# One core, attention and two expert layers: the attention stage's DMA issues put in another order

## The chip, the core and the metric

The kernel runs on one core of a Trainium2 chip, in one launch. The core has five engines, each with an instruction stream of its own that it works off strictly in order: TensorE (PE, matmuls; its weight loads are listed as PEld), VectorE (DVE), ScalarE (ACT), GpSimd (POOL) and SyncE (SP), which here does nothing but issue DMAs. They wait for one another and for DMAs at semaphores. A DMA is issued by SP and then moved by 16 DMA engines on their own; while SP waits for what one DMA needs, all DMAs behind it in its stream wait too. The metric is the device time of one execution in microseconds. Three runs of the kernel before took 801.37, 802.45 and 802.65 us; the median is 802.45.

## The reference

Attention over clusters, then two expert layers on its output, all in float32. Sizes: batch 2, 8 heads, 768 positions, head dimension 64, 16 centroids per head.

```python
q_assign = argmax(q_n @ c_n^T)        # cluster of each query, by normalised vectors
k_assign = argmax(k_n @ c_n^T)        # cluster of each key
scores = where(q_assign == k_assign, q @ k^T / sqrt(64), -1e9)
attn = exp(scores - max(scores)); attn /= sum(attn) + 1e-9
x = attn @ v                          # heads side by side: 1536 tokens x 512
h = x @ w_in                          # 512 -> 2048
x = ((a0 + a1 h + a2 h^2 + a3 h^3) / (1 + |b0||h| + |b1| h^2 + 1e-6)) @ w_out
x = (silu(x @ w_gate) * (x @ w_val)) @ w_o2       # 512 -> 1536 -> 512
```

## The kernel before, in words

Three stages follow one another: attention (the first 255 us of the profiled span), the first expert layer, the second expert layer. The change lies in attention alone.

Attention works on pairs of heads, 8 of them (`pairs`). A pair has 12 steps: 2 halves of the queries, 3 blocks of 128 queries in each, 2 heads. The main loop (line 617) runs over all 96 steps n; below, s = n mod 12 is the step within a pair and k = n // 12 the pair. All instructions go out in the order in which the loop writes them; the schedule is by hand and nothing reorders it. In each step:

- `scores` (369): four matmuls give 128 x 768 scores. q and k are split into a rounded part and a remainder, and stand in two tiles each: q1 and k1 hold 128 rows, q2 and k2 hold 64 rows of q or k and behind them 16 mask rows, a one-hot of the cluster times a large number, so that the mask comes out of the same matmuls.
- `maximum` (385, DVE) and `exponentials` (392, ACT) read the scores; the sum over each row falls out of the exponential. Two score tiles exist (`ps_s`).
- `transposes` (424, PE) turn the exponentials of earlier steps; ACT and DVE copy them to `pt`.

At steps 2 and 8 a *run* of 24 matmuls (`weighted`, 435) multiplies a finished half with v. It accumulates in `o_ps`, of which there is one only: the next run can't start before `normalised` (445, DVE) has read the last one. `normalised` gives x = o_ps * rb, and stands at step 0 and step 6 (in the first pair one step later). rb holds the reciprocals of the row sums, spread over the partitions. They come by a long way: `reciprocals` (401, DVE) and a transpose to `rs` at steps 2 and 8 (`spread`, 408, PE and ACT), a DMA from rs to a DRAM tile rd (line 415, also steps 2 and 8), and at steps 4 and 10 two DMAs from rd to rb with a broadcast (`bring_back`, 418). The half whose run stands at step 2 gets its reciprocals at step 2, rb at step 4, x at step 6, and the run at step 8 waits for that x.

During a pair the next one is made ready: its queries and keys are rounded and split on POOL (`halves_of`, 584: head one at steps 0 to 3, head two at 4 to 7), its clusters are found on DVE (`chain_of`, 559: steps 8 and 2), and the mask rows t3 are transposed on DVE at step 2 (`to_rows`, 357). Weight blocks for the later stages are loaded and prepared in some steps (`early`, 530).

The order of SP's stream is therefore the order in which these functions are called. Per pair, from the second on:

| step | SP's issues in the kernel before |
|---|---|
| 0 | sq and sk of the pair after next (`load_pair`, 187); q2 <- q1 of head one (273) |
| 2 | eight mask rows t3 -> q2 and k2 (365); rd <- rs (415) |
| 4 | rb <- rd, two (422); in most pairs a weight block (78); q2 <- q1 of head two (273) |
| 8 | rd <- rs |
| 10 | rb <- rd, two; v of both heads (192); q and k of both heads of the pair after next, four (181) |

In the first pair the mask rows go out at step 8 instead of 2, ahead of rd, and `load_pair` at step 4. The last pair has no pair to make ready, and so no mask rows, no rounded queries and no loads of q, k and v.

Of the kernel before, what the change touches and what calls it, by code (L numbers as in the profile page):

```python
# [20 lines left out]
def tile_kernel(ctx, tc, q_t, k_t, q_s, k_s, v_l, cent, w_in, w_out, a_co, b_co, w_gate, w_val, w_o2, out):  # L21
# [17 lines left out]
    def r32(ap):  # L39
        return ap.bitcast(F32)  # L40
# [76 lines left out]
    def block_start():  # L117
        n = len(started)
        if n < len(loads):
            key, f, src = loads[n]  # L120
            started.append(block_load(src[f]))
# [40 lines left out]
    heads = {}  # L162
    live = {}
    pairs = [(b, hp) for b in range(B) for hp in range(H // 2)]
    order = [(b, hp, half, i, e) for b, hp in pairs for half in range(2) for i in range(HB) for e in range(2)]
    PER = 2 * HB
# [5 lines left out]
    def x_tile(key):  # L172
        at = S * (n_x[0] % 6)
        n_x[0] += 1
        return xa[:, at:at + S]

    def load_qk(b, h):
        t = heads.setdefault((b, h), {})
        for key, src in (("xq", q_t), ("xk", k_t)):
            t[key] = x_tile(key)  # L180
            nc.sync.dma_start(out=t[key], in_=src[b, h])


    def load_pair(b, hp, keys=("sq", "sk")):
        for key in keys:
            live[key] = xs_p.tile([P, S], F32, tag=key, name=key)
            nc.sync.dma_start(out=live[key], in_=(q_s if key == "sq" else k_s)[b, hp])

    def load_v(b, h):
        t = heads[b, h]  # L190
        t["v"] = v_p.tile([P, NB, D], F32, tag="v", name="v")
        nc.sync.dma_start(out=t["v"], in_=v_l[b, h])
# [19 lines left out]
    def keep_warm(n, to, x=None):  # L212
        for _ in range(n):
            for j in range(HB):
                nc.tensor.transpose(to[:, j, :], ident if x is None else x[:, 0:P], ident)
# [47 lines left out]
    def tiles_qk(b, h):  # L263
        t = heads[b, h]
        for key in ("q1", "q2", "k1", "k2"):
            t[key] = qk_p.tile([P, S], F32R, tag=key, name=key)

    def q_hi(b, h):
        t = heads[b, h]
        if "q1" not in t:  # L270
            tiles_qk(b, h)
        nc.gpsimd.tensor_scalar(out=t["q1"], in0=t["xq"], scalar1=scale, scalar2=0.0, op0=ALU.mult, op1=ALU.add)
        nc.sync.dma_start(out=r32(t["q2"])[0:D, :], in_=r32(t["q1"])[0:D, :])

    def q_scale(b, h):
# [78 lines left out]
        sm = live["sm"]  # L354
        nc.scalar.activation(out=sm, in_=sm, func=AF.Identity, scale=msk[:, 0:1], bias=msk[:, 1:2])

    def to_rows(b, hp):
        del live["t1"], live["mx"]
        t3 = rb_p.tile([P, HALF], F32, tag="rb", name="t3")
        nc.vector.transpose(out=t3, in_=live.pop("sm").rearrange("p j c -> p (j c)"))  # L360
        for e in range(2):
            for m, key in enumerate(("q2", "k2")):
                for half in range(2):
                    g = 64 * m + 32 * half + NC * e
                    nc.sync.dma_start(  # L365
                        out=r32(heads[b, 2 * hp + e][key])[D:KM, half * HALF:(half + 1) * HALF], in_=t3[g:g + NC, :]
                    )

    def scores(b, hp, half, i, e):
        t = heads[b, 2 * hp + e]  # L370
        s_ps = ps_s.tile([P, S], F32, tag="s", name="s_ps")
        q0 = half * HALF + i * P
        qs = slice(q0, q0 + P)
        for lo, hi in CUT:
            nc.tensor.matmul(s_ps[:, lo:hi], t["q1"][:, qs], t["k1"][:, lo:hi], start=True, stop=False)  # L375
        if (b, hp, half, i, e) == order[0]:
            keep_warm(6, fill, oh[0])
        for lo, hi in CUT:
            nc.tensor.matmul(s_ps[:, lo:hi], t["q2"][0:KM, qs], t["k2"][0:KM, lo:hi], start=False, stop=True)  # L379
        if (i, e) == (0, 0):  # L380
            st = live["st", b, hp, half] = st_p.tile([P, 3, PER], F32, tag="st", name="st")
            nc.vector.memset(st[:, 2, :], 1e-9)
        live["s", b, hp, half, i, e] = s_ps

    def maximum(b, hp, half, i, e):
        st = live["st", b, hp, half]
        k = e * HB + i
        nc.vector.tensor_reduce(  # L388
            out=st[:, 0, k:k + 1], in_=live["s", b, hp, half, i, e], axis=AX.X, op=ALU.max, negate=True
        )  # L390
# [27 lines left out]
    def bring_back(b, hp, half):  # L418
        rd = live.pop(("rd", b, hp, half))
        rb = live["rb", b, hp, half] = rb_p.tile([P, HALF], F32, tag="rb", name="rb")  # L420
        for e in range(2):
            nc.sync.dma_start(out=rb[e * D:(e + 1) * D, :], in_=rd[e:e + 1, :].to_broadcast([D, HALF]))

    def transposes(b, hp, half, i, e, g, copy):
        p = live["p", b, hp, half, i, e] if g == 0 else live.pop(("p", b, hp, half, i, e))
        if (i, g) == (0, 0):
            live["pt", b, hp, half, e] = pt_p.tile([P, NB, HALF], F32, tag="pt", name="pt")
        pt = live["pt", b, hp, half, e]
        t_ps = t_tile("t_ps")
        for j in range(HB):  # L430
            kb = g * HB + j
            nc.tensor.transpose(t_ps[:, j, :], p[:, kb * P:(kb + 1) * P], ident)  # L432
        copy(out=pt[:, g * HB:(g + 1) * HB, i * P:(i + 1) * P], in_=t_ps)  # L433
# [82 lines left out]
    def q_rows(t, half):  # L516
        nc.scalar.activation(
            out=t["q2"][D:D + 32, cols[half]], in_=t["t3"][32 * half:32 * half + 32, :],
            func=AF.Identity, scale=MASKED, bias=msk[32 * half:32 * half + 32, 1:2],
        )  # L520
# [12 lines left out]
    def pair_of(k):  # L533
        b, hp = pairs[k + 1]
        return b, hp, (b, 2 * hp), (b, 2 * hp + 1)

    def loads_of(n):
        k, s = divmod(n, 2 * PER)
        if n == early[0] - 7 or n - 2 in early[:-1]:
            block_start()  # L540
        if s == (0 if k else 4) and k + 2 < len(pairs):
            load_pair(*pairs[k + 2])
        elif s == 10 and k + 1 < len(pairs):
            b, hp, a, c = pair_of(k)
            load_v(*a)
            load_v(*c)
            if k + 2 < len(pairs):
                b, hp = pairs[k + 2]
                load_qk(b, 2 * hp)
                load_qk(b, 2 * hp + 1)  # L550

    def sims_of(n):
        k, s = divmod(n, 2 * PER)
# [25 lines left out]
    def rows_of(n):  # L579
        k, s = divmod(n, 2 * PER)  # L580
        if k + 1 < len(pairs) and (n == 8 or n > 8 and s == 2):
            to_rows(*pairs[k + 1])

    def halves_of(n):
        k, s = divmod(n, 2 * PER)
# [22 lines left out]
    def run_of(m):  # L608
        for _ in range(m):
            if pv:  # L610
                step = pv.pop(0)
                weighted(*step)
                if step[3] == NB - 1:
                    return step[:3]

    finished = done = None
    for n in range(len(order) + 2):
        c = n % PER
        if n < len(order):
            scores(*order[n])  # L620
            maximum(*order[n])
        if n == 1:
            keep_warm(3, fill)
        for j, (lag, g, copy) in enumerate(TURNS[c]):
            if (n, j) == (len(order), 1):
                finished = run_of(NB)
            if n >= lag:
                transposes(*order[n - lag], g, copy)
                if g == 1 and (n - lag) % PER == PER - 1:
                    pv.extend([order[n - lag][:3] + (kb,) for kb in range(NB)])  # L630
        if n < len(order):
            exponentials(*order[n])
        if n == 1:
            q_rows(h1, 1)
            for t in (h0, h1):
                del t["t3"]
        if finished and (n == len(order) + 1 or c == (1 if n < 3 * PER else 0) and n < len(order)):
            normalised(*finished)
            finished, done = None, finished
        if c == RUN and n > PER:  # L640
            reciprocals(*order[n - 3][:3])
        elif n == len(order):
            reciprocals(*order[-1][:3])
        if c == 4 and n > PER:
            bring_back(*order[n - 5][:3])
        loads_of(n)
        sims_of(n)
        if c == RUN:
            finished = run_of(NB if n < LATE else NB // 2)
        if n == 8:  # L650
            rows_of(n)
        if n in early:
            block_shift(started[early.index(n)])
        chain_of(n)
        halves_of(n)
        if done and c == RUN:
            split_x(*done)
            done = None
        block_of(n)
        if n > 8:  # L660
            rows_of(n)
        if c == RUN and n > PER:
            spread(*order[n - 3][:3])
        elif n == len(order) + 1:
            spread(*order[-1][:3])
# [11 lines left out]
    with ExitStack() as mctx:  # L677
# [292 lines left out]
        for n in range(NS):  # L970
            t, f = seq[n][:2]
# [422 lines left out]
        j, c = 2 * u, 2  # L1394
# [61 lines left out]
```

## Time and profile before

| | |
|---|---|
| median of 3 runs | 802.45 us (801.37 to 802.65) |
| the profiled execution | 805.28 us |
| its span, first to last instruction | 803.5 us |
| PE busy | 776.2 us, 97% of the span |
| DVE, ACT, POOL busy | 603.9, 505.5, 455.3 us (75%, 63%, 57%) |
| mean granted TensorE clock | 0.984 of 2.4 GHz |
| mean DMA rate | 85 GB/s |

The profiled execution is one, and its own time is what its span is held against; the timed runs are others. An engine's share over the whole span is a mean over three stages with different limits, so the attention stage is read by itself. A busy PE is one whose matmuls overlap without a gap; it says nothing about the clock, which has a column of its own in the windows. Idle time in front of an instruction is put down to what came last before it started.

### The profile page before, as it was taken

Reading aid. Unit: us, or ns where it says so; the run is one execution under the profiler, and the core shown is the slowest. Engines: PE = TensorE matmul, PEld = TensorE weight load, DVE = VectorE, ACT = ScalarE, POOL = GpSimd, SP = SyncE. Lnnn points to the kernel's source line nnn. Section 1 sums busy time; section 2 is a strip of 40 time slices with the busy share of each in tenths; the row PEclk is TensorE's granted clock in tenths of the full one; section 3 lists DMA queues with packets and bytes.
Section 4 is the critical chain, followed back from the end, with each engine's and each line's share of the span. In section 5 each row is a group of like instructions: output and inputs, shape, how many; then the busy total and the mean of one; then the engine's idle time right before and its main releaser. Section 6 shows DMA issues by size and latency. Waiting matters only on the chain.

```text
span 803.5 us, 11575 instructions
## 1 busy us (share of the span) xinstructions
PE 776.2 (97%) x4119; PEld 646.9 (81%) x4119; DVE 603.9 (75%) x919; ACT 505.5 (63%) x959; POOL 455.3 (57%) x429
## 2 busy tenths in 40 slices
PE   8979889898899999999999999999999999999998
PEld 6756766576676888888888888899999999999997
DVE  6857778587576999988999999998576566656444
ACT  7756666485586778868777777666554544444331
POOL 6473874764922477666777777947344445434310
PEclk9998999899999999999999999999999999999999
DMA  7265354254122212112112111012221213120003
GB/s 218 72 201 180 90 181 162 55 173 160 56 93 73 68 65 78 56 50 79 53 53 78 53 54 52 28 52 80 80 78 56 76 53 106 53 79 27 1 36 122
DMA packets 27209, 67.94 MB, mean 85 GB/s; under 512 B 4464, under 2 KB 10832, under 8 KB 27152
## 3 DMA queue, kind: packets, MB, share of 16 engines
q1 hardware_dynamic: 27152, 67.21, 25.8%
q8 instruction: 32, 0.52, 0.3%
q14 instruction: 25, 0.20, 0.1%
HBM read 59.48 MB, written 3.19 MB: 78 GB/s over the span
## 4 chain that ended last, share of the span: by engine, by line
PE 84%; DVE 5%; ACT 4%; DMA 3%; POOL 2%; issue 1%; SPq 1%; DVEq 0%; POOLq 0%; ACTq 0%
PE c_ps L1046 23%; PE acc L782 14%; PE h_ps L726 14%; PE acc L1103 12%; PE o_ps L439 9%; PE t_ps L432 5%; PE s_ps L375 3%; PE s_ps L379 3%; DMA rb<-rd 2%; DVE st L388 2%; DMA rd<-rs 1%; ACT p L396 1%; POOL tmp L743 1%; DVE x L447 1%; SPq L365 1%
## 5 line engine op out<-in xcount | busy, mean ns | idle before, releaser
L1046 PE MATMUL c_ps<-r,wb 128*128 128x384 f32 x648 | 125.3, 336 | 0.0
L1046 PEld LDWEIGHTS c_ps<-r,wb 128*128 128x128 f32 x648 | 115.4, 188 | 6.0
L388 DVE TENSOR_REDUCE st<-s_ps 128x1 f32<-128x768 f32 x96 | 90.7, 953 | 28.5 <-PE s_ps L379 28.3
L396 ACT ACTIVATE p<-s_ps,st 128x768 f32<-128x768 f32 x96 | 86.9, 906 | 36.5 <-DVE st L388 35.7
L439 PE MATMUL o_ps<-pt,v 128*64 128x384 f32 x384 | 76.6, 552 | 20.0 <-DVE x L447 20.0
L743 POOL TENSOR_TENSOR tmp<-tmp 128x512 f32<-128x512 f32 x46 | 68.1, 1480 | 47.5 <-ACT tmp L742 47.1
L1054 ACT COPY tmp<-c_ps 128x384 f32<-128x384 f32 x60 | 28.9, 481 | 86.9 <-PE c_ps L1046 86.9
L439 PEld LDWEIGHTS o_ps<-pt,v 128*64 128x64 f32 x384 | 34.3, 154 | 58.0 <-issue 30.9
L1125 POOL TENSOR_TENSOR part<-tmp,part 128x512 f32<-128x512 f32 x18 | 23.4, 1298 | 101.2 <-ACT tmp L1124 101.2
L432 PE MATMUL t_ps<-ident,p 128*128 128x128 f32 x576 | 76.3, 272 | 0.5 <-DVE pt L433 0.5
L432 PEld LDWEIGHTS t_ps<-ident,p 128*128 128x128 f32 x576 | 66.0, 140 | 4.8 <-DVE pt L433 0.7
L782 PE MATMUL acc<-g,r 128*128 128x512 f32 x288 | 69.1, 389 | 0.2 <-ACT part L789 0.2
L766 POOL TENSOR_TENSOR g<-td,tmp 128x512 fp32r<-128x512 f32 x45 | 58.6, 1301 | 18.0 <-DVE td L761 18.0
L433 ACT COPY pt<-t_ps 128x384 f32<-128x384 f32 x128 | 56.7, 481 | 16.0 <-PE t_ps L432 13.7
L1057 DVE TENSOR_TENSOR tmp<-tmp,c_ps 128x384 f32<-128x384 f32 x40 | 22.2, 554 | 58.9 <-ACT tmp L1054 45.1
L1046 PE MATMUL c_ps<-r,xw 128*128 128x384 f32 x336 | 65.4, 337 | 0.0
L782 PEld LDWEIGHTS acc<-g,r 128*128 128x128 f32 x288 | 54.0, 188 | 11.8 <-ACT part L789 0.6
L1046 PEld LDWEIGHTS c_ps<-r,xw 128*128 128x128 f32 x336 | 60.0, 188 | 3.7
L726 PE MATMUL h_ps<-r 128*128 128x512 f32 x252 | 60.5, 390 | 0.0
L1103 PE MATMUL acc<-wb,g 128*128 128x512 f32 x216 | 59.4, 394 | 0.0
L375 PE MATMUL s_ps<-k,q 128*128 128x512 f32 x192 | 57.6, 381 | 1.3 <-ACT p L396 1.1
L726 PEld LDWEIGHTS h_ps<-r 128*128 128x128 f32 x252 | 47.1, 188 | 10.3 <-issue 0.6
(169 smaller groups left out, 1793.9 us busy)
## 6 DMA issues: line engine op xcount, KB each, us to landing
raw<-w_in_dram SPq DMA_DIRECT2D x16, 512.0 KB
raw<-w_out_dram SPq DMA_DIRECT2D x16, 512.0 KB
raw<-w_val_dram SPq DMA_DIRECT2D x12, 512.0 KB
raw<-w_gate_dram SPq DMA_DIRECT2D x12, 512.0 KB
raw<-w_o_dram SPq DMA_DIRECT2D x12, 512.0 KB
xa<-q_t_dram SPq DMA_DIRECT2D x14, 384.0 KB
xa<-k_t_dram SPq DMA_DIRECT2D x14, 384.0 KB
sq<-q_s_dram SPq DMA_DIRECT2D x8, 384.0 KB
```

The source lines that it names most:

```text
L375: nc.tensor.matmul(s_ps[:, lo:hi], t["q1"][:, qs], t["k1"][:, lo:hi], start=True, stop=False)
L388: nc.vector.tensor_reduce(out=st[:, 0, k:k + 1], in_=live["s", b, hp, half, i, e], axis=AX.X, op=ALU.max, negate=True)
L396: nc.scalar.activation(out=p, in_=live.pop(("s", b, hp, half, i, e)), func=AF.Exp, bias=st[:, 0, k:k + 1], accum_out=st[:, 1, k:k + 1],)
L432: nc.tensor.transpose(t_ps[:, j, :], p[:, kb * P:(kb + 1) * P], ident)
L433: copy(out=pt[:, g * HB:(g + 1) * HB, i * P:(i + 1) * P], in_=t_ps)
L439: nc.tensor.matmul(live["o", b, hp, half][e * D:(e + 1) * D, :], heads[b, 2 * hp + e]["v"][:, kb, :], live["pt", b, hp, half, e][:, kb, :] ...
L726: nc.tensor.matmul(h_ps, w[:, wi, cs], x[:, xi, cc, :], start=(n == 0), stop=(n == 3 * NCC - 1))
L743: spread.tensor_tensor(out=tq, in0=tq, in1=tr, op=ALU.add)
L766: eng.tensor_tensor(out=g[:, 1, :], in0=td, in1=tr, op=ALU.mult)
L782: nc.tensor.matmul(acc[c], w[:, wi, cs], g[:, gi, :], start=(first and m == 0), stop=(last and m == 2))
L1046: nc.tensor.matmul(live2[key], set_of[f][:, wi, a, cs], x[xi][:, kc, :], start=(first and n == 0), stop=(n == last), skip_group_check=True,)
L1103: nc.tensor.matmul(acc2[j, c], g[:, gi, c * P:(c + 1) * P], w[:, wi, :], start=(f % 2 == 0 and m == 0), stop=(f % 2 == 1 and m == 2),)
```

## The change

`to_rows` is cut in two: the transpose on DVE stays at step 2, and the eight DMAs become `send_rows`, at step 4 behind `bring_back` (in the first pair at step 8 as before). The DMA q2 <- q1 is taken out of `q_hi` and becomes `q_send`, at steps 5 and 9. The loads of q and k of the pair after next are spread: head one at step 5, head two at step 10. A new function `sends_of` is called in each step after `bring_back` and before `loads_of`. No other instruction is touched.

| step | SP's issues in the changed kernel, from the second pair on |
|---|---|
| 0 | sq and sk of the pair after next |
| 2 | rd <- rs |
| 4 | rb <- rd, two; eight mask rows; in most pairs a weight block |
| 5 | q2 <- q1 of head one; q and k of head one of the pair after next |
| 8 | rd <- rs |
| 9 | q2 <- q1 of head two |
| 10 | rb <- rd, two; v of both heads; q and k of head two of the pair after next |

```diff
--- before.py
+++ after.py
@@ -270,6 +270,9 @@
         if "q1" not in t:
             tiles_qk(b, h)
         nc.gpsimd.tensor_scalar(out=t["q1"], in0=t["xq"], scalar1=scale, scalar2=0.0, op0=ALU.mult, op1=ALU.add)
+
+    def q_send(b, h):
+        t = heads[b, h]
         nc.sync.dma_start(out=r32(t["q2"])[0:D, :], in_=r32(t["q1"])[0:D, :])
 
     def q_scale(b, h):
@@ -354,10 +357,14 @@
         sm = live["sm"]
         nc.scalar.activation(out=sm, in_=sm, func=AF.Identity, scale=msk[:, 0:1], bias=msk[:, 1:2])
 
-    def to_rows(b, hp):
+    def to_rows():
         del live["t1"], live["mx"]
         t3 = rb_p.tile([P, HALF], F32, tag="rb", name="t3")
         nc.vector.transpose(out=t3, in_=live.pop("sm").rearrange("p j c -> p (j c)"))
+        live["t3"] = t3
+
+    def send_rows(b, hp):
+        t3 = live.pop("t3")
         for e in range(2):
             for m, key in enumerate(("q2", "k2")):
                 for half in range(2):
@@ -544,10 +551,9 @@
             b, hp, a, c = pair_of(k)
             load_v(*a)
             load_v(*c)
-            if k + 2 < len(pairs):
-                b, hp = pairs[k + 2]
-                load_qk(b, 2 * hp)
-                load_qk(b, 2 * hp + 1)
+        if s in (5, 10) and k + 2 < len(pairs):
+            b, hp = pairs[k + 2]
+            load_qk(b, 2 * hp + (s == 10))
 
     def sims_of(n):
         k, s = divmod(n, 2 * PER)
@@ -579,7 +585,20 @@
     def rows_of(n):
         k, s = divmod(n, 2 * PER)
         if k + 1 < len(pairs) and (n == 8 or n > 8 and s == 2):
-            to_rows(*pairs[k + 1])
+            to_rows()
+        if n == 8:
+            send_rows(*pairs[1])
+
+    def sends_of(n):
+        k, s = divmod(n, 2 * PER)
+        if k + 1 < len(pairs):
+            b, hp, a, c = pair_of(k)
+            if s == 4 and k:
+                send_rows(b, hp)
+            elif s == 5:
+                q_send(*a)
+            elif s == 9:
+                q_send(*c)
 
     def halves_of(n):
         k, s = divmod(n, 2 * PER)
@@ -643,6 +662,7 @@
             reciprocals(*order[-1][:3])
         if c == 4 and n > PER:
             bring_back(*order[n - 5][:3])
+        sends_of(n)
         loads_of(n)
         sims_of(n)
         if c == RUN:
```

## Rows read from the trace of the kernel before

**Rows 1.** The page, costliest groups: busy us, mean ns, idle before, what ended it.

```profile
L439 PE MATMUL o_ps<-pt,v 128*64 128x384 f32 x384 | 76.6, 552 | 20.0 <-DVE x L447 20.0
```

**Rows 2.** Waits over the whole span: us in total, times, longest us.

```profile
POOL q L272 <- DMA xa<-q_t_dram: 58.7, 5, 16.0
...
DVE x L447 <- DMA rb<-rd: 27.3, 6, 5.7
```

**Rows 3.** Timeline of PE: the runs of line 439.

```profile
59.58 6.82 PE L439 MATMUL o_ps<-pt,v 128*64 128x384 f32 x24 [4.31 <-DVE x L447]
...
74.95 4.09 PE L439 MATMUL o_ps<-pt,v 128*64 128x384 f32 x24
...
90.63 4.16 PE L439 MATMUL o_ps<-pt,v 128*64 128x384 f32 x24 [2.25 <-DVE x L447]
...
119.85 5.71 PE L439 MATMUL o_ps<-pt,v 128*64 128x384 f32 x24 [3.08 <-DVE x L447]
...
151.17 7.10 PE L439 MATMUL o_ps<-pt,v 128*64 128x384 f32 x24 [3.63 <-DVE x L447]
...
183.25 5.85 PE L439 MATMUL o_ps<-pt,v 128*64 128x384 f32 x24 [2.95 <-DVE x L447]
...
214.10 5.86 PE L439 MATMUL o_ps<-pt,v 128*64 128x384 f32 x24 [3.56 <-DVE x L447]
...
241.07 2.16 PE L439 MATMUL o_ps<-pt,v 128*64 128x384 f32 x12
```

**Rows 4.** Windows: stretch, length, busy us (count) by engine, PEclk, DMA share, GB/s.

```profile
59.50:66.40 6.90, 6.82 (x26) 3.24 (x26) 5.18 (x11) 2.44 (x5) 3.89 (x7) 0.60 0.01 2
93.00:116.80 23.80, 23.77 (x166) 18.02 (x162) 19.81 (x32) 18.08 (x42) 17.01 (x22) 1.00 0.43 144
38.50:48.00 9.50, 9.29 (x63) 6.26 (x62) 6.87 (x12) 6.52 (x16) 3.15 (x5) 1.00 0.88 311
48.50:51.00 2.50, 2.50 (x20) 2.30 (x19) 2.50 (x5) 2.43 (x7) 2.33 (x4) 1.00 0.99 224
```

**Rows 5.** Timeline of all engines in the third pair, steps 2 to 8.

```profile
79.28 0.26 ACT L413 COPY rs<-r_ps 6x128 f32<-6x128 f32 x1 [0.96 <-PE r_ps L411]
...
87.89 0.49 PE L306 MATMUL sim<-sk,ct 128*32 128x384 f32 x2
...
88.02 0.84 POOL L272 TENSOR_SCALAR q<-xa 128x768 fp32r<-128x768 f32 x1
...
90.02 0.56 DVE L447 TENSOR_TENSOR x<-o_ps,rb 128x384 f32<-128x384 f32 x1 [3.64 <-DMA rb<-rd]
```

**Rows 6.** Timeline of SP in the same stretch.

```profile
80.06 1.19 SPq L365 DMA_DIRECT2D q<-t  x2
...
85.14 0.42 SPq L415 DMA_DIRECT2D rd<-rs  x1
...
86.52 1.12 SPq L422 DMA_DIRECT2D rb<-rd  x2
...
87.69 0.58 SPq L78 DMA_DIRECT2D raw<-w_in_dram  x1
```

**Rows 7.** Timeline of SP: rd at step 8 there, and in the last pair.

```profile
95.32 0.29 SPq L415 DMA_DIRECT2D rd<-rs  x1
...
233.11 0.28 SPq L415 DMA_DIRECT2D rd<-rs  x1
```

**Rows 8.** Timeline of DVE: x of the half with run at step 8.

```profile
102.06 0.55 DVE L447 TENSOR_TENSOR x<-o_ps,rb 128x384 f32<-128x384 f32 x1
```

**Rows 9.** Timeline of DVE: lines 349 and 95 in two places each.

```profile
28.05 1.07 DVE L349 TENSOR_TENSOR sm<-wt,mx 128x384 f32<-128x384 f32 x1
...
43.42 0.56 DVE L349 TENSOR_TENSOR sm<-wt,mx 128x384 f32<-128x384 f32 x1
...
78.34 1.20 DVE L95 SCALAR_TENSOR_TENSOR c<-raw,c 128x512 uint32<-128x512 uint32 x1
...
231.77 0.69 DVE L95 SCALAR_TENSOR_TENSOR c<-raw,c 128x512 uint32<-128x512 uint32 x1
```

## Prediction

> **What bounds the kernel now.** I read the page's groups of instructions first, then the waits, then TensorE's instructions in order of time around each wait, then the DMA queue's own instructions beside them. A row of a timeline is: start, duration, engine, line, operation, tiles, count, and in brackets the idle time before it and what ended it. TensorE (PE) is busy 97% of the span, so a gain can only come from its few idle stretches or from what makes it slow. The group of the weighted sums (line 439) holds 20.0 us of idle time, all of it ended by the product x of line 447 on VectorE (DVE) [rows 1]. DVE in turn waited 27.3 us, 6 times, for the broadcast rows rb that come back by DMA [rows 2].
>
> In order of time that is six places, one in each pair from the second on, always at step 8 of 12: idle 4.31, 2.25, 3.08, 3.63, 2.95 and 3.56 us, together 19.8 us [rows 3]. The run of 24 matmuls behind the wait is stretched too: 6.82, 4.16, 5.71, 7.10, 5.85 and 5.86 us, against 4.09 us for the same run at step 2 [rows 3]. Only the one after the shortest wait (2.25 us) is at its normal length. The granted clock says why: over the first of these stretched groups of 24 it is 0.60 in the mean, so a good part of it was at 1.2 GHz, and in a stretch between two waits it is 1.00, that is 2.4 GHz [rows 4]. So a wait costs twice: 19.8 us of idling, and 35.50 - 6 x 4.09 = 11.0 us of slow matmuls.
>
> Why rb is late is seen in the DMA queue (SPq, which issues strictly in order). The reciprocals' row rs is written by ScalarE at 79.28 to 79.54 [rows 5]. Its transfer to DRAM, rd, is issued only at 85.14, because the eight issues of mask rows stand in front of it from 80.06 on [rows 6]: 5.6 us lost. From rd's issue to x it then takes 90.02 - 85.14 = 4.88 us [rows 5, 6].
>
> **The change part by part.** No computing instruction is added or removed, and no byte; issues change places.
>
> *Mask rows behind the reciprocals.* At step 2 the queue now holds nothing between the loads of step 0 and rd, so rd can go at about 79.6 in the pair shown, and x could start at 79.6 + 4.88 = 84.5. The run is due when what stands ahead of it is done: the last matmul ahead of the run ends at 87.89 + 0.49 = 88.4 [rows 5], and x takes 0.56 and must be over by then, so it has to start by about 87.8. It is 3.3 us early. DVE itself is free for x earlier than it is now: it stood idle in front of x. The last pair is the same step without mask rows: rd is issued at 233.11 and the run at 241.07 starts without a wait [rows 7, 3]. So I let all six waits go whole, and with them the extra length of the matmuls behind: -19.8 - 11.0 = -30.8 us.
>
> A second way to the same number: from the run at 90.63 to the start of the next idle stretch (119.85 - 3.08 = 116.77) is 26.1 us, one pair without a wait. The stretch from the first idle start (59.58 - 4.31 = 55.27) to the end of the last stretched group (214.10 + 5.86 = 219.96) is 164.7 us; five clean pairs and one run are 5 x 26.1 + 4.09 = 134.6 us. That is 30.1 us less. I take 30.5.
>
> What keeps TensorE from finding another wait: in the stretch from 93.0 to 116.8, which has a step-2 run in it and no wait, PE is busy 23.77 of 23.80 us while DVE has 19.81 and ScalarE 18.08 [rows 4]. These engines have room to follow at 26.1 us a pair.
>
> *Where the eight mask rows go.* They take 85.14 - 80.06 = 5.1 us of issue time [rows 6]. At step 4 they stand behind the two issues of rb, at about 82 to 87 in the pair shown. Their reader is the first score of the next pair, at step 0, some ten us later. I cost them at nothing; what hides them is the matmuls of steps 5 to 11. In the first pair they stay at step 8, so nothing changes there.
>
> *Rounded queries (the DMA from q1 to q2).* They leave at steps 5 and 9 instead of 0 and 4. The wait on GpSimd (POOL) that SPq had in front of rd is gone: POOL rounds the first head at step 0. The second head's copy now stands between rd of step 8 and rb of step 10. POOL has written it at 88.02 + 0.84 = 88.86, and rd of that step goes at 95.32 [rows 5, 7], so SPq finds it done. Its issue fits into the time in which SPq waits for rd to land (85.14 to 86.52 at step 2, rd's own issue in it [rows 6]). In the first pair this copy goes out just behind the first rd, and its reader is the second score of the next pair, four steps later: between nothing and 0.5 us (its own issue), once, and I take nothing, four steps being some 5 us.
>
> *Loads spread.* One head's queries and keys (2 x 384 KB) move from step 10 to step 5. POOL waited 58.7 us in all for the queries [rows 2]; it will start the rounding at step 0 at once, and its work moves forward. POOL bounds nothing, so this saves nothing by itself. Its price lies at step 8: the weight block (512 KB), the rounded queries (192 KB) and the two loads, 1.5 MB, are issued between about 87 and 89.3, just ahead of the other half's rd. That half's x has some room: rd at 95.32 allows x at 100.2, and it ran at 102.06 [rows 7, 8], so rd may be 1.9 us late for nothing. DMA moved 311 GB/s over a full stretch, and 224 GB/s in the poorest one in which the engines were still busy throughout, with mask rows among the loads [rows 4]. With data from 88.4 on (1.4 us behind the issue, as rb follows rd), 1.5 MB last to 93.2 or to 95.1. The clean pair issues that rd at 88.4 + 4.09 + 0.6 = 93.1, so it is late by 0.1 to 2.0 us, inside the room or 0.1 us past it: between nothing and 6 x 0.1 = 0.6 us, and I take nothing.
> The Trainium skill ("DMA: Bandwidth & Descriptors", Queues, rings and completion order) says that each DMA engine takes its descriptors in ring order, which speaks against putting loads there: by it the small rd waits for the whole 1.5 MB. By it the sum loses nothing as long as the poorer rate holds, and 6 us for each further us that the 1.5 MB take. It is the mechanism of the third rival below, where the loss from a lower rate is worked out.
>
> **Sum.** Span 803.5 - 30.5 = 773.0 us. The profiled execution took 805.28, 1.8 more than its span, so 774.8; the median of the timed runs is 802.45, 2.8 below the profiled execution. With the same difference: 772.0 us.
>
> **Rivals.**
> *First: DVE becomes the bound and part of the gain stays away.* POOL's work now falls beside DVE's operations of step 2, and DVE is slower then: the one-hot comparison (line 349) took 1.07 and 0.56 us, the bit operation of line 95 took 1.20 and 0.69 us in two places [rows 9]. If both always take the longer time and nothing absorbs it, that is 1.0 us per pair, 6 us in all: 778 us; with rb late now and then beside a burst of loads as well, up to 790. Against it: DVE's 19.81 of 23.8 us in a stretch without a wait [rows 4].
> *Second: the change doesn't do what it says.* The wait is put down to rb, but an instruction that waits for several things may wait for another. Then the order of SPq moves nothing: 802 us. Against it: the last pair, without mask rows, has no wait [rows 3].
> *Third, on the slow side: the wait moves from step 8 to step 2.* The loads at step 5 hold back rd of step 8, so x of the other half is late. From 1.9 us of delay on, each further us is a us of idle in six runs; from some 3 us of idle on, 2.2 us of slow matmuls come on top (the mean excess of the five stretched groups). What is gained per pair is 5.1 us, so the change loses from a delay of 1.9 + 2.9 = 4.8 us on. For that, 1.5 MB would have to take 9.6 us, 156 GB/s, well below the 224 seen. With a delay of 7 us: 6 x (5.1 + 2.2) = 44 us back, 816 us.
>
> **Chances.** Forecast (769 to 775 us): 0.75. First rival (775 to 790): 0.15. Second: 0.04. Third: 0.04. Still faster than 769: 0.02. The range 768 to 781 holds the forecast and over half of the first rival. About 0.2%, 1.6 us, is what a measurement of this kernel can tell from no change. Faster: 0.75 + 0.15 + 0.02 = 0.92; same: 0.04; slower: 0.04.
>
> **What would show it.** Right: SPq issues rd within 1 us of the run's end at step 2, with the mask rows behind rb; no idle in front of any run of line 439 at step 8; all these runs at 4.1 us and the granted clock at 1.00 from 50 to 220; attention over some 30 us earlier and the stages behind it as long as now. Wrong: x still waiting for rb at step 6 (second rival); DVE without idle time and TensorE waiting for maxima or exponentials at steps 3 to 8 (first); idle in front of the runs at step 2, with rd or rb landing late (third).

## The result, 775.13 us against 802.45, and the profile after

The changed kernel took 774.57 to 776.95 us in five runs, median 775.13; its ratio to the kernel before is 0.9661, 95% interval 0.9643 to 0.9678. The forecast was 772.0 us, between 768 and 781. The profiled execution took 775.13 us, its span 773.4 us (forecast 774.8 and 773.0). Line numbers above 272 are shifted: line 439 of before is 446, line 447 is 454, line 365 is 372, 415 is 422 and 422 is 429. In the kernels in which q2 <- q1 stays where it was, they are three lower (443, 451, 419, 426).

The page's group of the weighted sums, to be held against [rows 1]: idle time 20.0 us to 0.2 us, and the mean matmul 552 to 491 ns.

```profile
L446 PE MATMUL o_ps<-pt,v 128*64 128x384 f32 x384 | 65.7, 491 | 0.2 <-DVE x L454 0.2
```

TensorE's timeline (start, length, and in brackets the idle time before), the runs at step 8 that answer to [rows 3], and one row more. All six are 4.09 us long and none has a bracket. The last row is new: 1.62 us of idle in front of the scores of step 11 of the seventh pair, behind an exponential.

```profile
54.73 4.09 PE L446 MATMUL o_ps<-pt,v 128*64 128x384 f32 x24
...
80.73 4.09 PE L446 MATMUL o_ps<-pt,v 128*64 128x384 f32 x24
...
106.73 4.09 PE L446 MATMUL o_ps<-pt,v 128*64 128x384 f32 x24
...
132.71 4.09 PE L446 MATMUL o_ps<-pt,v 128*64 128x384 f32 x24
...
158.69 4.09 PE L446 MATMUL o_ps<-pt,v 128*64 128x384 f32 x24
...
183.89 4.09 PE L446 MATMUL o_ps<-pt,v 128*64 128x384 f32 x24
...
192.86 0.61 PE L382 MATMUL s_ps<-k,q 128*128 128x512 f32 x2 [1.62 <-ACT p L403]
```

Windows (stretch, length, busy us of PE, PEld, DVE, ACT, POOL with counts, granted clock, DMA share, GB/s), as [rows 4]: two whole pairs are 52.0 us with TensorE busy throughout at full clock, so a pair takes 26.0 us. The second row is the end of attention and what follows it. What lies behind the last run of attention takes as long as before: 803.5 - 259.9 = 543.6 us before (run at 255.84, 4.09 long) and 773.4 - 229.8 = 543.6 us after (run at 225.70).

```profile
66.00:118.00 52.00, 52.00 (x358) 37.70 (x357) 41.88 (x75) 39.08 (x89) 38.35 (x52) 1.00 0.55 175
220.00:274.00 54.00, 53.55 (x248) 41.40 (x245) 45.55 (x68) 39.77 (x69) 28.23 (x24) 1.00 0.25 82
```

SP's timeline in the third pair, as [rows 6]: the run at step 2 ends at 67.36 + 4.09 = 71.45; rd goes 0.5 us later, rb at 73.20, then the mask rows and the weight block. At step 8 rd goes at 85.34, with the queries behind it.

```profile
71.97 0.28 SPq L422 DMA_DIRECT2D rd<-rs  x1
73.20 1.09 SPq L429 DMA_DIRECT2D rb<-rd  x2
74.40 1.18 SPq L372 DMA_DIRECT2D q<-t  x2
...
79.41 0.59 SPq L78 DMA_DIRECT2D raw<-w_in_dram  x1
...
85.34 0.28 SPq L422 DMA_DIRECT2D rd<-rs  x1
85.72 0.50 SPq L276 DMA_DIRECT2D q<-q  x1
87.18 1.11 SPq L429 DMA_DIRECT2D rb<-rd  x2
```

### The profile page after: what moved, and what is told of

Read it like the earlier page. It is cut to its first block, busy times and chain, and to the rows that moved or that the text cites. A ratio compares the mean times of both kernels' runs of the same rounds, so it can differ in the third digit from the quotient of the medians.

```text
span 773.4 us, 11590 instructions
## 1 busy us (share of the span) xinstructions
PE 764.4 (99%) x4119; PEld 638.7 (83%) x4119; DVE 595.8 (77%) x919; ACT 504.8 (65%) x959; POOL 453.3 (59%) x429
## 4 chain that ended last, share of the span: by engine, by line
PE 89%; DVE 4%; ACT 3%; POOL 2%; issue 1%; DMA 1%; SPq 0%; POOLq 0%; DVEq 0%; ACTq 0%
PE c_ps L1066 23%; PE acc L802 15%; PE h_ps L746 14%; PE acc L1123 13%; PE o_ps L446 8%; PE t_ps L439 7%; PE s_ps L382 4%; PE s_ps L386 4%; DVE st L395 1%; PE sim L309 1%; POOL tmp L763 1%; ACT p L403 1%; DMA raw<-w_in_dram 1%; PE w_ps L215 1%; POOL k L494 0%
## 5 line engine op out<-in xcount | busy, mean ns | idle before, releaser
L403 ACT ACTIVATE p<-s_ps,st 128x768 f32<-128x768 f32 x96 | 86.9, 906 | 10.3 <-DVE st L395 9.5
L446 PE MATMUL o_ps<-pt,v 128*64 128x384 f32 x384 | 65.7, 491 | 0.2 <-DVE x L454 0.2
L446 PEld LDWEIGHTS o_ps<-pt,v 128*64 128x64 f32 x384 | 26.1, 137 | 35.0 <-issue 31.4
```

Of the source, the lines that this page charges most:

```text
L403: nc.scalar.activation(out=p, in_=live.pop(("s", b, hp, half, i, e)), func=AF.Exp, bias=st[:, 0, k:k + 1], accum_out=st[:, 1, k:k + 1],)
L446: nc.tensor.matmul(live["o", b, hp, half][e * D:(e + 1) * D, :], heads[b, 2 * hp + e]["v"][:, kb, :], live["pt", b, hp, half, e][:, kb, :] ...
```

## Experiments

All times are medians of four to six runs; ratios are to the kernel before, timed beside them (802.53 to 802.84 us).

**The mask rows alone.** Of the change only this stays; queries at steps 0 and 4, all loads at step 10:

```diff
     def q_hi(b, h):
         ...
+        nc.sync.dma_start(out=r32(t["q2"])[0:D, :], in_=r32(t["q1"])[0:D, :])
     def sends_of(n):
             if s == 4 and k:
                 send_rows(b, hp)
-            elif s == 5: q_send(*a)
-            elif s == 9: q_send(*c)
     # loads_of, step 10
+            load_qk(b, 2 * hp); load_qk(b, 2 * hp + 1)
```

> Of the change only the mask rows: their eight issues go to step 4 behind rb, while the rounded queries stay at steps 0 and 4 and all four loads at step 10. Theory (the late rd is the whole cause): all six waits at step 8 go, every run of 24 matmuls takes 4.1 us, 774 to 777 us, like the full change. Rival (the loads matter too): the 3.2 MB issued at step 10 and the copy of the queries that waits for POOL at step 0 still stand in front of rd, so waits of 1 to 3 us stay at step 8 in most pairs: 782 to 792 us.

778.25 us, 0.9699 (0.9683 to 0.9714): between the two. Five of the six waits are gone, the first is 1.47 us. SP's timeline of that pair says why: rd left at 46.22, right behind the run, but rb followed only at 52.32. SP waited 6.1 us for three kilobytes to land, where the changed kernel needs 1.2 to 1.6 us at this step (its two traces). About 3.4 MB had been issued since step 10 (v, the loads, sq and sk, the queries' copy, a weight block) and were still being moved: the windows' DMA share was 1.05 from 46 to 49 us, against 0.32 in the changed kernel.

```profile
46.22 0.34 SPq L419 DMA_DIRECT2D rd<-rs  x1
52.32 1.09 SPq L426 DMA_DIRECT2D rb<-rd  x2
```
```profile
46.00:49.00 3.00, 3.00 (x25) 2.77 (x24) 2.20 (x3) 2.27 (x6) 2.91 (x5) 1.00 1.05 364
```

In the other pairs it was 1.2 to 3.7 us from rd to rb at this step, and no run waited. In TensorE's timeline, that wait and the one of the seventh pair, which has grown to 2.53 us:

```profile
56.28 4.16 PE L443 MATMUL o_ps<-pt,v 128*64 128x384 f32 x24 [1.47 <-DVE x L451]
...
196.24 0.62 PE L379 MATMUL s_ps<-k,q 128*128 128x512 f32 x2 [2.53 <-ACT p L400]
```

**The other two parts without the mask rows.** The changed kernel with `send_rows` called right after `to_rows` at step 2, in front of rd:

```diff
     def rows_of(n):
         ...
             to_rows()
-        if n == 8:
-            send_rows(*pairs[1])
+            send_rows(*pairs[k + 1])
     def sends_of(n):
         ...
-            if s == 4 and k:
-                send_rows(b, hp)
```

> The other two parts of the change without the mask rows: queries sent at steps 5 and 9, loads at steps 5 and 10, but the eight mask rows at step 2 in front of rd as before. Theory: the rows alone hold rd back by about 5 us, so the six waits of 2 to 4 us stay and the time stays at 799 to 804 us. Rival: the wait for POOL in front of the rows and the burst of loads are a good part of the delay; then the waits shrink by half or more, below 792 us.

789.90 us, 0.9846 (0.9823 to 0.9869). My theory was wrong here: nearly half of the gain (12.6 us) comes without moving the mask rows. The waits are still there, but 1.24 to 2.79 us in place of 2.25 to 4.31. In the third pair rd goes at 78.81, 5.5 us behind the run's end (69.21 + 4.09), against 6.1 us before [rows 3, 6]; the second pair gains most: its eight mask rows took 7.3 us to issue while the burst of loads was being moved, and take 5.2 us here. And a shorter wait is worth more than its length: behind 1.24 to 1.58 us the run keeps its 4.16 us; only two of the six are stretched, behind 2.79 and 2.27 us. TensorE's timeline, one of each:

```profile
84.19 4.16 PE L446 MATMUL o_ps<-pt,v 128*64 128x384 f32 x24 [1.55 <-DVE x L454]
...
197.41 5.86 PE L446 MATMUL o_ps<-pt,v 128*64 128x384 f32 x24 [2.27 <-DVE x L454]
```

**A filler against the falling clock.** The kernel before with transposes that nobody reads in front of the run:

```diff
+        if n % (2 * PER) == 8 and 8 < n < 84:
+            keep_warm(10, t_tile("wf"))
         if c == RUN:
             finished = run_of(...)
```

> The kernel before with 30 extra transposes that nobody reads on TensorE in front of each of the six runs at step 8 (9 transposes took 0.98 us, so 3.3 us each time). x is as late as before; TensorE only no longer idles while it waits. Theory (waiting and the fall of the clock are two separate costs, 19.8 and 11.0 us): the waits stay, the six runs take 4.1 us each at a granted clock of 1.00, and where the wait was shorter than 3.3 us up to 1 us is lost: 791 to 794 us. Rival (the runs are stretched by something else, late operands or the PSUM bank): the runs stay at 5.7 to 7.1 us and the filler costs what it costs: 802 to 806 us.

795.32 us, 0.9908 (0.9893 to 0.9922), a little above the range. All six runs take 4.09 to 4.16 us and the mean clock of the whole execution is 1.000 (before: 0.984). So the length of the runs was the clock's alone, and the clock's fall followed the idling. x is as late as before, added over the six pairs (1.9 us later in the second, up to 0.9 us earlier in the others). The timelines of one pair, DVE and TensorE: x is over at 88.31 + 0.56 = 88.87, but the filler of 3.50 us holds the run until 90.03. In four of the six it overruns x, by 3.1 us in all; I had allowed up to 1 us.

```profile
88.31 0.56 DVE L447 TENSOR_TENSOR x<-o_ps,rb 128x384 f32<-128x384 f32 x1 [3.65 <-DMA rb<-rd]
```
```profile
86.60 3.50 PE L215 MATMUL wf<-ident 128*128 128x128 f32 x30
90.03 4.09 PE L439 MATMUL o_ps<-pt,v 128*64 128x384 f32 x24
```

**rd first, mask rows between rd and rb.** One swap in the loop of the kernel before:

```diff
-        if n > 8:
-            rows_of(n)
         if c == RUN and n > PER:
             spread(*order[n - 3][:3])
         ...
+        if n > 8:
+            rows_of(n)
```

> The kernel before with one pair of statements swapped: at step 2 rd goes first and the eight mask rows follow it, so they stand in front of rb. Loads and queries as before. Theory (x follows rb's issue by 3.5 us whatever is first): rb goes about 1.4 us earlier than before, since only rd's landing is now hidden behind the rows; the waits shrink to 0.5 to 2.5 us, most are too short for the clock to fall, 783 to 790 us. Rival (getting rd out early is what counts): all waits go, 774 to 778 us.

789.88 us, 0.9832 (0.9805 to 0.9859), at the upper end of what was expected. rb, not rd, has to be early: in SP's timeline of the third pair rd goes at 74.93, 0.5 us behind the run, rb 5.7 us later; in TensorE's, 0.95 us of wait are left in that pair, up to 2.85 in the others.

```profile
74.93 0.29 SPq L415 DMA_DIRECT2D rd<-rs  x1
...
80.60 1.23 SPq L422 DMA_DIRECT2D rb<-rd  x2
```
```profile
84.73 4.16 PE L439 MATMUL o_ps<-pt,v 128*64 128x384 f32 x24 [0.95 <-DVE x L447]
```

**More loads in front of rd of step 8.** The changed kernel, timed again in this series (774.85 us, 0.9654 with 0.9637 to 0.9671), and with both heads' loads at step 5:

```diff
-        if s in (5, 10) and k + 2 < len(pairs):
+        if s == 5 and k + 2 < len(pairs):
             b, hp = pairs[k + 2]
-            load_qk(b, 2 * hp + (s == 10))
+            load_qk(b, 2 * hp)
+            load_qk(b, 2 * hp + 1)
```

> The changed kernel as it is, beside the other kernels of this series: 774.5 to 777 us, no other difference.

> The changed kernel with the loads of both heads at step 5, so that 0.79 MB more (2.5 us at 311 GB/s) stand in front of rd of step 8. Theory (small transfers wait behind the loads issued before them, the mechanism of the third rival): from rd's issue to rb's issue at step 8 to 10 it takes 3 to 4.5 us in place of the 1.24 to 1.84 us of the changed kernel, x at step 0 is 0 to 1 us late, the time is 1 to 5 us above the changed kernel: 776 to 780 us. Rival (rd does not wait behind loads): 1.2 to 1.9 us from rd to rb as now, and the time of the changed kernel within 0.7 us.

777.33 us, 0.9690 (0.9670 to 0.9710), 2.5 us above the changed kernel: the third rival's mechanism, at a small price. From rd of step 8 to rb it now takes 2.3 to 5.0 us in the second to sixth pairs (the changed kernel in its two traces: 1.2 to 2.2 us; the expectation's 1.84 was not its longest). In the worst pair x is 1.74 us late for DVE and the run at step 2 waits 1.10 us; the clock holds. SP, DVE and TensorE:

```profile
138.14 0.28 SPq L422 DMA_DIRECT2D rd<-rs  x1
...
143.09 1.11 SPq L429 DMA_DIRECT2D rb<-rd  x2
```
```profile
146.72 0.56 DVE L454 TENSOR_TENSOR x<-o_ps,rb 128x384 f32<-128x384 f32 x1 [1.74 <-DMA rb<-rd]
```
```profile
147.33 3.12 PE L446 MATMUL o_ps<-pt,v 128*64 128x384 f32 x18 [1.10 <-DVE x L454]
```

**Loads or queries?** The mask rows with one of the other two parts each: first the loads spread (queries as before), then the queries moved (all loads at step 10).

```diff
 # rows and loads: q_hi issues q2 <- q1 itself, and
-            elif s == 5: q_send(*a)
-            elif s == 9: q_send(*c)
 # rows and queries: in loads_of
-        if s in (5, 10) ...: load_qk(b, 2 * hp + (s == 10))
+        if s == 10 ...: load_qk(b, 2 * hp); load_qk(b, 2 * hp + 1)
```

> Mask rows at step 4 and loads spread over steps 5 and 10, rounded queries at steps 0 and 4 as before. With the mask rows alone the time was 778.25 us, with the whole change 775.13 and 774.85. Theory (the loads make the difference: in the kernel with the rows alone rb went 6.1 us behind rd, at 52.3, while the burst of step 10 drained): 774.5 to 775.6 us. Rival (the queries in front of rd make it): 777 to 779 us.

> Mask rows at step 4 and rounded queries at steps 5 and 9, all four loads at step 10 as before. Theory (the loads make the difference): 777 to 779 us, with rb some 4 to 6 us behind rd at step 2 of the second pair. Rival (the queries make it): 774.5 to 775.6 us.

774.42 us (0.9654, 0.9630 to 0.9679) and 777.64 us (0.9690, 0.9667 to 0.9712). Behind the rows the loads make the rest of the gain and the queries none that can be measured. SP's timeline of the second pair with the loads at step 10: 4.0 us from rd to rb. No run waited for it there, nor in any other pair.

```profile
45.81 0.28 SPq L422 DMA_DIRECT2D rd<-rs  x1
49.84 1.09 SPq L429 DMA_DIRECT2D rb<-rd  x2
```

So it is not a late rb that costs the time with the loads at step 10. TensorE idles in front of scores instead, behind an exponential, where a weight block is prepared: 0.54 us at 62.44 and 2.69 us in the seventh pair, in place of none and 1.62 us. DVE was slower there: lines 91 and 95 took 0.66 and 1.36 us, against 0.43 and 0.69 us in the changed kernel, because POOL was at work until 192.1; in the changed kernel POOL idled from 187.9 to 190.9. TensorE, DVE and POOL with the loads at step 10, then DVE of the changed kernel:

```profile
194.69 0.61 PE L382 MATMUL s_ps<-k,q 128*128 128x512 f32 x2 [2.69 <-ACT p L403]
```
```profile
191.32 1.36 DVE L95 SCALAR_TENSOR_TENSOR c<-raw,c 128x512 uint32<-128x512 uint32 x1
```
```profile
191.09 1.05 POOL L467 TENSOR_TENSOR r<-x,r 128x384 fp32r<-128x384 f32 x1
```
```profile
190.16 0.69 DVE L95 SCALAR_TENSOR_TENSOR c<-raw,c 128x512 uint32<-128x512 uint32 x1
```

The traces of all kernels say the same: the mean of line 95 in attention is 930 to 1040 ns in the five with all loads at step 10 (POOL waits 25 to 59 us in all for the queries' loads there) and 693 ns in each of the seven with the loads moved (no such wait). Among them are two pairs of kernels that differ in the loads alone: 971 and 693 ns with the queries as before, 1040 and 693 ns with the queries moved.

**The new wait of 1.62 us.** In the changed kernel, SP issues a weight block in the seventh pair at 184.30, behind the mask rows; ScalarE waits 2.53 us for it at 188.57 and DVE sits idle for 4.44 us, then holds maxima back. In this pair the block is shifted four steps after its issue; a block issued at step 4 of the third to sixth pairs has ten. SP, ACT and DVE of the changed kernel:

```profile
184.30 0.59 SPq L78 DMA_DIRECT2D raw<-w_in_dram  x1
```
```profile
188.57 0.68 ACT L82 ACTIVATE raw<-raw 128x512 f32<-128x512 f32 x1 [2.53 <-DMA raw<-w_in_dram]
```
```profile
189.70 0.43 DVE L91 TENSOR_SCALAR c<-raw 128x512 uint32<-128x512 uint32 x1 [4.44 <-ACT rs L420]
```

The edit moves the block in front of the mask rows:

```diff
     def sends_of(n):
         ...
             if s == 4 and k:
+                if n - 2 in early[:-1]:
+                    block_start()
                 send_rows(b, hp)
     def loads_of(n):
         ...
+        ahead = s == 4 and 0 < k < len(pairs) - 1
-        if n == early[0] - 7 or n - 2 in early[:-1]:
+        if n == early[0] - 7 or n - 2 in early[:-1] and not ahead:
             block_start()
```

> The changed kernel with the weight block of step 4 issued between rb and the mask rows instead of behind them. In the trace of the changed kernel TensorE idles 1.62 us once, at 191.2, behind ScalarE that waited for a weight block issued at 184.30, and DVE that sat idle 4.44 us. Theory (the rows now delay that block, and the step-8 wait no longer covers it): the idle of 1.62 us goes, 1.3 to 1.8 us faster than the changed kernel, 773.0 to 774.0 us. Rival (the block is late for another reason, or the next wait takes its place): within 0.5 us of the changed kernel, 774.6 to 775.6 us.

773.08 us, 0.9632 (0.9620 to 0.9645), all its runs at 772.82 to 773.13, below every run of the changed kernel (774.57 to 776.95): the best version, though the intervals of the ratios still overlap a little. SP issues the block at 178.01, ScalarE shifts it at 185.65 without a wait, and from 184 to 198 TensorE is busy throughout (changed kernel: 12.38 of 14 us).

```profile
178.01 0.59 SPq L78 DMA_DIRECT2D raw<-w_in_dram  x1
178.71 1.18 SPq L372 DMA_DIRECT2D q<-t  x2
```
```profile
184.00:192.00 8.00, 8.00 (x56) 5.47 (x53) 5.71 (x10) 5.62 (x13) 5.48 (x7) 1.00 0.32 81
192.00:198.00 6.00, 6.00 (x43) 4.54 (x43) 5.16 (x10) 5.54 (x13) 1.85 (x4) 1.00 0.43 157
```

With, on top, the last two blocks one step earlier:

```diff
+        last = early[-3:-1]
-        if n == early[0] - 7 or n - 2 in early[:-1] and not ahead:
+        if n == early[0] - 7 or n - 1 in last or n - 2 in early[:-3] and not ahead:
```

> The kernel with the weight block ahead of the mask rows, and the last two blocks of attention one step earlier (steps 9 and 3 of the last two pairs). In that kernel TensorE still idles 0.5 us once, behind a block near the end of attention. Theory: that idle goes, 772.3 to 772.8 us. Rival (the block issued at step 9 now holds back rb of step 10): a new wait at the next run, 773.1 us or more.

773.17 us, 0.9634 (0.9617 to 0.9651): no change. The idle of 0.54 us behind an exponential is still there, and no new wait came at the next run. ScalarE's and DVE's timelines show why: the shift of that block (line 82) follows the exponentials without a wait for a DMA, and DVE waits 1.43 us for it. So the load is not what is late. That the place of the shift in ScalarE's order is, was not tried.

```profile
210.74 0.66 ACT L82 ACTIVATE raw<-raw 128x512 f32<-128x512 f32 x1
```
```profile
211.49 0.43 DVE L91 TENSOR_SCALAR c<-raw 128x512 uint32<-128x512 uint32 x1 [1.43 <-ACT raw L82]
```

## Why the prediction was right, and where its parts were not

*The six waits and the stretched matmuls (-19.8 and -11.0 us).* Right, in place and size. All six are gone, the runs are at 4.09 us, and the span fell by 30.1 us (forecast 30.5). That these are two costs is shown by the filler: it left x as late as it was, added over the six, and took the second cost alone. Its 7.2 us and the 3.1 us of overrun make 10.3. That the span fits to 0.4 us is partly luck: the new wait takes 1.6 of the 30.8 us back, and 0.9 us were gained that no term names; about 0.5 of them lie before the first run of step 2 (at 41.85 before, 41.38 after, but 41.77 in the second trace of the changed kernel).

*The room of x.* I had 3.3 us at step 2 and 1.9 us at step 8. With the mask rows alone rb came 6.1 - 1.24 = 4.9 us later than an undisturbed 1.24 and TensorE waited 1.47 us, so the room was 3.4 us; 2.8 us later (rows and queries) cost no wait. With both loads at step 5, a delay of 4.99 - 1.24 = 3.75 us from the third pair's rd left DVE waiting 1.55 us: 2.2 us of room, and 1.8 to 2.2 us in the next three pairs. TensorE lost less than that: its run behind that x waited 0.92 us, so 2.8 us of delay were free for it, and not 1.9.

*"POOL bounds nothing, so this saves nothing by itself" (the loads).* This step failed. Spreading the loads is worth 2.5 to 3.8 us behind the mask rows (778.25 and 777.64 against 775.13, 774.85 and 774.42), and with the queries it is worth 12.6 us where the mask rows stay. With the mask rows moved it works in two ways. One is what I had not looked at, a burst at step 10 in front of rd of step 2; but that cost a wait only once, 1.47 us, and only with the queries in their old place as well. The other is POOL itself: when the loads come late, POOL still rounds while DVE prepares a weight block, DVE takes longer, and the scores wait (in the trace with the loads at step 10, 0.54 us once and 1.1 us more in the seventh pair). What the burst does in the kernel before, and what the queries' copy does there, was not tried one by one. The 4.88 us that I took for a clean way from rd to x were of a pair in which the burst had drained while the mask rows went out; that the longer ways without them fitted into the room was luck. And the last pair, which I took for the same step without mask rows, has no loads and no queries either, so it could not tell the three apart.

*Costs taken at nothing.* The mask rows at step 4 and the queries cost TensorE nothing by themselves. But moved as they were, the eight issues push the weight block of step 4 later, and the wait at step 8 that used to cover it is gone: in the seventh pair it is issued 2.8 us ahead of the run before (211.30 [rows 3: 214.10]) and 0.4 us behind its start after. That made the 1.6 us, which I had not seen.

*From the span to the median.* The mis-sized term of the sum. I carried the 2.8 us between the profiled execution (805.28) and the median over to the changed kernel; there the profiled execution is the median. Most of the 2.8 us was clock: six timed executions of the kernel before with a mean clock of 0.984 or 0.985 took 803.6 to 805.6 us, those at 0.986 to 0.989 took 800.3 to 803.6. The profiled one had 0.984, and against 0.987 that is 0.003 x 803 = 2.4 us, an estimate. The changed kernel has no wait left behind which its clock fell in the profiled execution (1.000, as in all but one of its five runs; that one, 0.997, took 776.95 us), so nothing was to be taken off: 774.8 us would have been the forecast, 0.3 us from the measured. As it was, the time lies just above the forecast's own 769 to 775 us, in the interval that I had given to the first rival, but not by that rival's mechanism.

*Rivals.* The second is out by the trace. The third works as a mechanism (2.5 us with twice the loads) and stays far from its price of 44 us for a delay of 7 us. The first came out the other way round: in the changed kernel DVE's operations met POOL less than before, while its mechanism is at work where the loads stay at step 10. Groups of DVE in attention (count, busy us, mean ns, idle before), first of the changed kernel, then of the kernel before:

```profile
L95 DVE SCALAR_TENSOR_TENSOR c<-raw,c 128x512 uint32<-128x512 uint32 x9 | 6.2, 693 | 0.3
...
L352 DVE TENSOR_TENSOR sm<-wt,mx 128x384 f32<-128x384 f32 x7 | 4.4, 631 | 0.2
```
```profile
L95 DVE SCALAR_TENSOR_TENSOR c<-raw,c 128x512 uint32<-128x512 uint32 x9 | 8.4, 930 | 0.3
...
L349 DVE TENSOR_TENSOR sm<-wt,mx 128x384 f32<-128x384 f32 x7 | 5.5, 790 | 0.2
```

POOL no longer waits for the queries' loads [rows 2] and starts a pair's rounding earlier. The two pairs of kernels above that differ in the loads alone show that this is why DVE meets it less.

## What to carry to other kernels

In a queue that issues in order, follow the one small transfer whose landing an engine waits for, and count both what is issued in front of it and how many bytes are still being moved then: here the eight issues were worth 24 us over six pairs (mask rows alone), and more loads in front 2.5 us (both heads at step 5). A prefetch also sets when the engine that reads it works, and so beside whom: ask that of an engine that bounds nothing, too. A wait on TensorE costs more than its length when the clock falls behind it, so that shortening a wait can pay more than the time taken off. A profiled execution with a lower clock than the timed ones has time in it that the change will not give back a second time. When a stall goes, look for the loads whose lateness it covered.

## What the runs showed of the hardware

- Eight DMAs of 24 KB took SP 5.0 us to issue in most pairs, 0.6 us each, up to 6.2 us in some, and 7.3 us in the kernel before while a burst of loads was being moved. The 192 KB of the queries took 0.5 us and a weight block of 512 KB 0.6 us (184.99 and 184.30 in the changed kernel): the count sets the time, not the bytes.
- A 3 KB transfer took 1.24 us from its issue to the next issue that waits for it on a quiet queue. It took 1.2 to 2.2 us with 1.0 to 1.5 MB issued just before it (the changed kernel, step 8 of the second to sixth pairs), 2.3 to 5.0 us with 1.7 to 2.2 MB (both heads at step 5), and 6.1 us with 3.4 MB (mask rows alone).
- In these traces the run of 24 matmuls behind an idle stretch of TensorE of up to 1.58 us kept its 4.1 to 4.2 us. Behind 2.27, 2.67 and 2.79 us it took 5.86, 5.85 and 5.51 us, behind 2.25 [rows 3], 2.73 (behind the filler) and 2.85 us it took 4.09 to 4.16 us; behind each of the longer ones, 2.95 to 4.31 us, it took 5.7 to 7.1 us. Of two idle stretches in front of scores, 2.53 us was followed by a granted clock of 0.76 over 7 us (mask rows alone, 196 to 203) and 2.69 us by 1.00 (loads at step 10).
- DVE's operations with two inputs in SBUF are shorter when POOL is not at work: line 95 0.69 us against 1.20 us [rows 9]; POOL was rounding at 78.34 and idle at 231.77. Line 91, which has one input, is longer too: 0.43 us, and 0.66 us beside POOL (loads at step 10). The Trainium skill ("SBUF — State Buffer", Who interferes with whom) says that a DVE instruction with two SBUF inputs contends with a GpSimd instruction that reads SBUF; the means of 930 and 693 ns before and after agree.
